# An mLSTM cell followed by a gated feed-forward: the second product of two of four batches by seven half-width block products in place of eight

## The chip, the core and the metric

The kernel runs on one core of one Trainium2 chip. The metric is device time in microseconds of one launch. Before the change three runs took 549.52, 550.34 and 550.58 us, a median of 550.34 us. The profiled execution spans 549.5 us with a mean granted TensorE clock of 0.993.

## What is computed

There are four batches, eight heads, 768 time steps and a head size of 40. An mLSTM cell gives, for each batch and time step, a row of 8 x 40 = 320 numbers. These 3072 rows then go through a feed-forward with 2048 inner units, and this second part is what the change is about:

```python
# x: 3072 x 320, w_in: 320 x 2048, w_out: 2048 x 320, all float32
h = x @ w_in
g = h * np.cos(h)
return (g @ w_out).astype(np.float32)
```

## The kernel before, in words

**Chunks and blocks.** Time is cut into six chunks of 128 steps (`NC = 6`, index `c`). A chunk of one batch is a tile of 128 rows, so a chunk has four tiles, one per batch. The 2048 inner units are sixteen blocks of 128 (`NF = 16`), taken two at a time (`f2` from 0 to 7, `e` = 0 and 1 within a pair).

**First product.** `Up(c, f2)` computes h for one pair of blocks and all four batches, transposed: 128 inner units on the partitions and 4 x 128 time steps along the free axis. Each of the two blocks fills one PSUM bank of 512 float32, of which there are two in the pool `ps_u`, so the next `Up` needs both back. From these banks ScalarE rounds (`near`, L621), VectorE takes the rest (`rest`, L624), ScalarE takes the sine (`sin`, L629), and VectorE multiplies (`gate`, L633). The result `gs[c, 2 * f2 + e]` is a 128 x 512 tile in SBUF: inner units by (batch, time). The factor of two pi and the cosine are folded into the scaling.

**Second product.** `down(c, f2)` (L637 to L649) adds, for both blocks of a pair, g times w_out to the four output tiles of the chunk. Each output tile of one batch is 128 time steps by 320 columns and sits in a PSUM bank of its own for the whole chunk (`po[c]`, pool `ps_o`, four banks). A call is eight matmuls: for each block and batch, the 128 x 128 slice of g is the stationary operand and the 128 x 320 block of w_out the moving one. In the last call of a chunk (f2 = 7) the eight are sorted by batch, and each finished bank is copied by ScalarE to SBUF (L648, tile `o_sb`, two buffers) and sent out by DMA (L649).

**Order of the work.** The order on every engine is the program's order; it is written by hand in `both_parts(c, b)` (L789 to L899), called for each chunk and each b from 0 to 3. A call has two halves. The first half issues `Up(c, 2b)`, then pieces of the mLSTM cell of the next chunk (scores, weights, the exponents `decay_exponents` for the cell after that, the exponential `decay`), and then `down` of the pair before. The second half issues `Up(c, 2b + 1)`, the end of the cell, and `down(c, 2b)`. So each `down` is issued one half later than its `Up`. The last pair of chunk c - 1 is done in the first half of `both_parts(c, 0)`, and for the last chunk after the loops (L907).

Within a first half the queues hold, in this order: ScalarE `near`, `sin`, the exponential of `decay` (L379), then the output copies of `down` if it closes a chunk; VectorE `rest`, `weigh` (L451), the subtraction of `decay_exponents` (L370), `gate`, later `normalize_turned`; GpSimd the selection of `decay_exponents` (L371), on which the exponential of `decay` waits, and `weigh_k` (L392); TensorE `Up`, `scores` (L445), `down`, `values_turned` (L482, L488), then the next `Up`. From chunk 5 on there are no cells left, and a half holds `Up` and `down` alone.

**Weights.** w_in and w_out arrive as 64-bit floats and are converted in chunk 0, by `parts` on ScalarE and `join` on VectorE and GpSimd. The tiles `bits` (pools `pb` and `pc`) and `wt` (pool `p2`) serve that conversion and lie idle afterwards.

Of the kernel before, what the change touches and what calls it, by code (L numbers as in the profile page):

```python
# [11 lines left out]
FP = mybir.dt.float32  # L12
# [4 lines left out]
OP = mybir.AluOpType  # L17
# [12 lines left out]
def kernel(  # L30
# [20 lines left out]
    nc = tc.nc  # L51

    B, H, S, D = q.shape
    C = 128
# [4 lines left out]
    DM = H * D  # L59
    DFF = moe_w_in.shape[1]  # L60
    NF = DFF // 128
# [13 lines left out]
    p2 = ctx.enter_context(tc.tile_pool(name="p2", bufs=2))  # L75
    p3 = ctx.enter_context(tc.tile_pool(name="p3", bufs=3))
    p4 = ctx.enter_context(tc.tile_pool(name="p4", bufs=4))
    pb = ctx.enter_context(tc.tile_pool(name="pb", bufs=5))
    pc = ctx.enter_context(tc.tile_pool(name="pc", bufs=3))
# [3 lines left out]
    ps_o = ctx.enter_context(tc.tile_pool(name="ps_o", bufs=4, space=bass.MemoryType.PSUM))  # L83
# [15 lines left out]
    p1 = ctx.enter_context(tc.tile_pool(name="p1", bufs=1))  # L99
# [20 lines left out]
    w_out_sb = wp.tile([128, NF, DM], FP, name="w_out_sb")  # L120
# [11 lines left out]
    def parts(dst, bits):  # L132
        n = dst.shape[1]
        hi, lo = bits[:, 0:n, 1], bits[:, 0:n, 0].bitcast(U32)
        t = p2.tile([128, WQ], I32, name="wt", tag="wt")[:, 0:n]
        m = p2.tile([128, WQ], I32, name="wm", tag="wm")[:, 0:n]

        nc.scalar.activation(out=t.bitcast(FP), in_=hi.bitcast(FP), func=AF.Abs)

        nc.scalar.activation(out=m, in_=lo, func=AF.Copy, scale=2.0 ** -29)  # L140
        return dst, hi, t, m
# [164 lines left out]
    def sigmoid(c, bs=slice(0, B)):  # L306
        o = sig[c][:, bs.start * DM:bs.stop * DM]
        nc.scalar.activation(out=o, in_=o, func=AF.Sigmoid)
# [51 lines left out]
    def psum_o():  # L360
        return ps_o.tile([128, HP, C], FP, name="pm", tag="o")

    def cols(n, j, width):
        c, b = divmod(n, B)
        return tab[:, c, j, ts(b, H)].unsqueeze(2).to_broadcast([128, H, width])


    def decay_exponents(n):
        E = Es[n]
        nc.vector.tensor_tensor(out=E, in0=E, in1=cols(n, 0, C), op=OP.subtract)  # L370
        nc.gpsimd.affine_select(out=E, in_=E, compare_op=OP.is_ge, fill=1.0e30, base=0,  # L371
                                pattern=[[0, H], [1, C]], channel_multiplier=-1)
# [5 lines left out]
    def decay(n):  # L378
        nc.scalar.activation(out=Es[n], in_=Es[n], func=AF.Exp, scale=-1.0)  # L379
# [9 lines left out]
    def weigh_k(n):  # L389
        if n < N - B:  # L390
            kw = p2.tile([128, H, D], FP, name="kw", tag="kw")
            nc.gpsimd.tensor_tensor(out=kw, in0=ks[n % NB][:, :, 0:D], in1=cols(n, 1, D), op=OP.mult)  # L392
            kws[n] = kw
# [44 lines left out]
    def scores(n):  # L438
        pool, tag = psum(n)
        qT, kT = qkT[n]  # L440
        ps = [pool.tile([128, HP, C], FP, name="ps", tag=tag) for _ in range(2)]
        for p in range(HP):
            for j in range(2):
                r = slice(64 * j, 64 * j + (64 if n < TURNED else D))
                nc.tensor.matmul(ps[j][:, p], kT[r, p], qT[r, p], start=True, stop=True)  # L445
        pss[n] = ps

    def weigh(n):
        for j in range(2):
            w = Es[n].rearrange("p (a j) t -> p a j t", j=2)[:, :, j]  # L450
            nc.vector.tensor_tensor(out=w, in0=pss[n][j], in1=w, op=OP.mult)  # L451

    def values_kept(n):

        pool, tag = (ps_o, "o") if n == B else psum(n)
        heads_of[n] = None
        if n >= B:
            pq = pool.tile([128, H, D1], FP, name="pq", tag=tag)
            for p in range(HP):
                nc.tensor.matmul(pq[:, 2 * p:2 * p + 2].rearrange("p j d -> p (j d)"), qkT[n][0][:, p],  # L460
                                 st[n % B][:, p].rearrange("p j d -> p (j d)"), start=True, stop=True)
            heads_of[n] = pq
# [136 lines left out]
    gs, po = {}, {}  # L599

    class Up:
# [29 lines left out]
        def gate(self, e):  # L631
# [2 lines left out]
                                           op0=OP.mult, op1=OP.mult)  # L634
            gs[self.c, 2 * self.f2 + e] = g

    def down(c, f2):  # L637
        if f2 == 0:
            po[c] = [ps_o.tile([128, DM], FP, name="po", tag="o") for _ in range(B)]

        order = [(f, b) for f in (2 * f2, 2 * f2 + 1) for b in range(B)]
        if f2 == NF // 2 - 1:
            order.sort(key=lambda fb: fb[1])
        for f, b in order:
            nc.tensor.matmul(po[c][b], gs[c, f][:, ts(b, C)], w_out_sb[:, f], start=(f == 0), stop=(f == NF - 1))  # L645
            if f == NF - 1:
                o = p2.tile([128, DM], FP, name="o_sb", tag="o_sb")
                nc.scalar.copy(out=o, in_=po[c][b])  # L648
                nc.sync.dma_start(out=out[b * S + c * C:b * S + (c + 1) * C], in_=o)  # L649


    pw, pmu = (ps_u.tile([128, HP, C], FP, name=name, tag="up") for name in ("pw", "pmu"))
# [1 line left out]
    def warm(k, bank=None):  # L654

        for _ in range(k):
            nc.tensor.matmul(bank or pw, nil, nil.unsqueeze(1).to_broadcast([128, HP, 128]), start=True, stop=True)
# [122 lines left out]
    def out_parts():  # L780
        p, piece = outs.pop(0)
        return p, parts(*piece)

    def out_join(p, h, last=None):
        join(*h, last)
        if p + 3 < NF // 2:
            outs.append((p + 3, weights_out(p + 3)))

    def both_parts(c, b):  # L789

        n = (c + 1) * B + b
        cell = n < N
        begin = c == b == 0
        more = cell and n + 1 < N
        f2 = 2 * b
        up = Up(c, f2)
        if cell:  # L800
            scores(n)
            if begin:
                values_kept(n)

                warm(6, psum_o())
        for e in range(2):
            up.near(e)
        if begin:
            weigh(n)
        for e in range(2):  # L810
            up.rest(e)
        if cell and not begin:
            weigh(n)
        if begin or more and c > 0:
            decay_exponents(n + 1)
        for e in range(2):
            up.sin(e)
            up.gate(e)
        if c == 0 and b == 1:
            sigmoid(1, slice(1, B))  # L820
        if b == B - 1 and c + 2 < NC:
            sigmoid(c + 2)
        h = ()
        if begin:
            h = out_parts()
            w = parts(*pieces.pop(0))
        else:
            if c == 0:
                out_join(*out_parts())
            if pieces:  # L830
                join(*parts(*pieces.pop(0)))
        if begin or more and c > 0:
            decay(n + 1)
        elif more:
            decay_by_bias(n + 1)
        if f2 > 0:
            down(c, f2 - 1)
        elif c > 0:
            down(c - 1, NF // 2 - 1)
        if cell:  # L840
            if n + 2 < N:
                load(n + 2)
            if n < TURNED:
                if not begin:
                    values_kept(n)
                values(n)
                normalize(n)
            else:
                values_turned(n)
            if begin:  # L850
                out_join(*h, nc.vector)
            if TURNED <= n + 2 < N:
                load_G(n + 2)
            if n + 3 < N:
                load_E(n + 3)
            if b == B - 2 and c + 2 < NC:
                load_o(c + 2)
            if n >= TURNED:
                normalize_turned(n)
            fade(n)  # L860
        h = w if begin else ()
        if not begin:
            sin_next()
        if pieces and not begin:
            h = parts(*pieces.pop(0))
        up = Up(c, f2 + 1)
        if cell:
            seam(n)
        for e in range(2):
            up.near(e)  # L870
        for e in range(2):
            up.rest(e)
        if cell and n < TURNED:
            seam_out(n)
        if h:
            join(*h)
        if cell:
            state(n)
        for e in range(2):
            up.sin(e)  # L880
            up.gate(e)
        if more:
            weigh_k(n + 1)
        if pieces:
            join(*parts(*pieces.pop(0)))
        down(c, f2)
        if pieces:
            join(*parts(*pieces.pop(0)))
        if c == 0:
            if b + 2 < B:  # L890
                pieces.extend(weights_in(b + 2))
            h = out_parts()
        if more and n + 1 < TURNED:
            turn(n + 1)
            turn_out(n + 1, c > 0)
        elif more:
            turn_blocks(n + 1)
        if c == 0:
            out_join(*h)  # L899
# [38 lines left out]
```

## Time and profile before

| what | value |
|---|---|
| TensorE busy | 538.8 us of the 549.5 |
| VectorE busy | 355.9 us |
| ScalarE busy | 264.4 us |
| GpSimd busy | 76.7 us |
| matmul records at L645 (the second product) | 768 |
| matmul records at L613 and L616 (the first product) | 384 and 192 |
| first and last copy of an output tile, L648 | 143.8 and 545.6 us |
| output copies of chunks 1, 2, 3 begin | 228.41, 312.92, 397.43 us |

The profile gives for each engine the time that it was busy, for each source line the instructions and their mean duration, and, in the timeline, runs of equal instructions with the start, the time from the first start to the last end, and how many there were. "PE" is TensorE's matmuls and "PEld" its weight loads, "DVE" is VectorE, "ACT" ScalarE, "POOL" GpSimd. The second product has 16 blocks x 24 tiles = 384 matmuls in the program and 768 records: each float32 matmul is recorded as two passes, each with a weight load of its own. Durations of matmuls overlap, since they are pipelined; the distance from one start to the next is what a pass costs in a full stream.

### The profile page before, as it was taken

The page shows a single profiled execution, that of the slowest core. Times are in us where ns is not written, and L with a number is a line of the kernel's source. Part 1 is how long each engine was busy: PE and PEld are TensorE (multiplying, and loading weights), DVE is VectorE, ACT ScalarE, POOL GpSimd, SP SyncE. Part 2 cuts the span into 40 slices and gives each one's busy share as a digit, 9 for nine tenths or more (in the row PEclk, how much of TensorE's full clock was granted, in tenths as well). Part 3 has the DMA queues.
Part 4 walks back from the last instruction along what each step waited for, and adds up shares of the span by engine and source line. Part 5 has one row for each costly group of instructions (what it writes and reads, how often), then busy time and mean ns, then how long its engine had stood idle before and what let it go on. Part 6 is the DMA issues. An engine that isn't in the chain of part 4 may idle for free.

```text
span 549.5 us, 9153 instructions
## 1 busy us (share of the span) xinstructions
PE 538.8 (98%) x3395; PEld 317.4 (58%) x3395; DVE 355.9 (65%) x692; ACT 264.4 (48%) x420; POOL 76.7 (14%) x112
## 2 busy tenths in 40 slices
PE   9989899999999999999999999999999999999997
PEld 6865566665565565565565555555655655555554
DVE  5876987968777677677667667667666665232311
ACT  4868795775632544543435344427335323331312
POOL 5531433523110100101101101100000000000000
PEclk9979999999999999999999999999999999999999
DMA  9999985851265651166625076635075000100001
GB/s 143 206 226 221 239 220 145 189 124 33 77 142 129 148 124 36 50 136 138 151 75 107 26 158 139 143 78 110 4 173 109 8 14 12 51 1 1 0 0 50
DMA packets 134509, 56.83 MB, mean 103 GB/s; under 512 B 72080, under 2 KB 130528, under 8 KB 134464
## 3 DMA queue, kind: packets, MB, share of 16 engines
q1 hardware_dynamic: 134320, 56.04, 46.0%
q8 instruction: 27, 0.44, 0.3%
q0 software_dynamic: 96, 0.18, 0.2%
q14 instruction: 18, 0.15, 0.1%
q10 hardware_dynamic: 48, 0.02, 0.0%
HBM read 50.00 MB, written 6.21 MB: 102 GB/s over the span
## 4 chain that ended last, share of the span: by engine, by line
PE 85%; DVE 5%; DMA 4%; SPq 3%; POOL 1%; ACT 1%; issue 1%; DVEq 0%; ACTq 0%; POOLq 0%
PE po L645 37%; PE pup L613 28%; PE pup L616 8%; PE hp L488 3%; PE ps L445 3%; PE hp L482 2%; PE pu L580 1%; DMA E<-M_d 1%; SPq L327 1%; PE pt L426 1%; SPq L129 1%; DMA qs<-in_q_dram 1%; DMA bits<-in_moe_w_out_dram 1%; DMA M_d<-M_rows 1%; DMA bits<-in_moe_w_in_dram 1%
## 5 line engine op out<-in xcount | busy, mean ns | idle before, releaser
L645 PE MATMUL po<-w_out_sb,g 128*128 128x320 f32 x768 | 219.3, 439 | 1.3 <-POOL w_out_sb L149 1.0
L645 PEld LDWEIGHTS po<-w_out_sb,g 128*128 128x128 f32 x768 | 142.0, 190 | 67.0 <-issue 8.3
L613 PE MATMUL pup<-xT,w_in_sb 128*128 128x512 f32 x384 | 175.5, 599 | 0.9 <-POOL w_in_sb L149 0.6
L621 ACT ACTIVATE n<-pup 128x512 int32<-128x512 f32 x96 | 52.0, 593 | 214.3 <-PE pup L616 214.3
L624 DVE SCALAR_TENSOR_TENSOR n<-pup,n 128x512 f32<-128x512 f32 x96 | 61.9, 686 | 135.1 <-ACT n L621 135.0
L613 PEld LDWEIGHTS pup<-xT,w_in_sb 128*128 128x128 f32 x384 | 71.2, 191 | 77.6 <-issue 63.9
L629 ACT ACTIVATE n<-n 128x512 f32<-128x512 f32 x96 | 58.8, 630 | 12.1 <-DVE n L624 12.1
L633 DVE SCALAR_TENSOR_TENSOR g<-pup,n 128x512 f32<-128x512 f32 x96 | 61.7, 685 | 1.7
L371 POOL TENSOR_SCALAR_AFFINE_SELECT E<-E 128x1024 f32<-128x1024 f32 x19 | 20.8, 1094 | 292.9 <-DVE E L370 273.6
L616 PE MATMUL pup<-xT,w_in_l 64*128 64x512 f32 x192 | 54.2, 641 | 0.0
L616 PEld LDWEIGHTS pup<-xT,w_in_l 64*128 64x128 f32 x192 | 14.4, 184 | 36.4 <-issue 35.6
L451 DVE TENSOR_TENSOR E<-ps,E 128x512 f32<-128x512 f32 x48 | 30.7, 680 | 6.1 <-PE ps L445 6.1
L379 ACT ACTIVATE E<-E 128x1024 f32<-128x1024 f32 x21 | 22.2, 1058 | 21.7 <-POOL E L371 17.2
L410 DVE STREAM_TRANSPOSE t<-qs 128x512 f32<-128x512 f32 x32 | 32.3, 1087 | 0.0
L445 PEld LDWEIGHTS ps<-t,t 40*128 40x128 f32 (+1 forms) x384 | 25.1, 188 | 9.7 <-issue 8.9
L445 PE MATMUL ps<-t,t 40*128 40x128 f32 (+1 forms) x384 | 25.8, 274 | 0.0
L370 DVE TENSOR_TENSOR E<-E,tab 128x1024 f32<-128x1024 f32 x19 | 23.1, 1216 | 0.4 <-DMA E<-M_d 0.4
L379 ACT ACT_TABLE_LOAD x18 | 23.1, 1283 | 0.3
L778 ACT ACT_TABLE_LOAD x18 | 23.1, 1283 | 0.3
L502 DVE STREAM_TRANSPOSE room<-hp 128x128 f32<-128x128 f32 x32 | 8.6, 306 | 22.5 <-PE hp L488 22.5
L488 PE MATMUL hp<-E,vs 128*32 128x128 f32 x512 | 17.3, 276 | 0.0
L417 DVE STREAM_TRANSPOSE room<-o 128x256 f32<-128x256 f32 x32 | 17.2, 618 | 0.0
(128 smaller groups left out, 428.9 us busy)
## 6 DMA issues: line engine op xcount, KB each, us to landing
E<-M_d SPq DMA_DIRECT2D x22, 512.0 KB
bits<-in_moe_w_in_dram SPq DMA_DIRECT2D x40, 128.0 KB
bits<-in_moe_w_out_dram SPq DMA_DIRECT2D x8, 640.0 KB
room<-G_d SPq DMA_DIRECT2D x32, 128.0 KB
ks<-in_k_dram SPq DMA_DIRECT2D x24, 160.0 KB
vs<-in_v_dram SPq DMA_DIRECT2D x24, 160.0 KB
out_dram<-o_sb SPq DMA_DIRECT2D x24, 160.0 KB
qs<-in_q_dram SPq DMA_DIRECT2D x32, 80.0 KB
```

Source lines behind the costliest of these rows:

```text
L379: nc.scalar.activation(out=Es[n], in_=Es[n], func=AF.Exp, scale=-1.0)
L410: nc.vector.transpose(out=dst.rearrange("r p (t x) -> r p x t", x=T4), in_=src.rearrange("r p (x d) -> r p x d", x=T4)[:, :, :, 0:32])
L445: nc.tensor.matmul(ps[j][:, p], kT[r, p], qT[r, p], start=True, stop=True)
L451: nc.vector.tensor_tensor(out=w, in0=pss[n][j], in1=w, op=OP.mult)
L488: nc.tensor.matmul(hps[n][j][ts(p, 32), half], vs[n % NB][:, h, lo:lo + DA], Es[n][:, h], start=False, stop=True, skip_group_check=True)
L613: nc.tensor.matmul(pu, w_in_sb[:, i, ts(block(f2, e), 128)], x(i), start=(i == 0), stop=False)
L616: nc.tensor.matmul(pu, w_in_l[r, f2], x(NK, r), start=False, stop=True)
L621: nc.scalar.activation(out=self.n[e], in_=self.pu[e], func=AF.Copy, bias=0.25)
L624: nc.vector.scalar_tensor_tensor(out=self.n[e].bitcast(FP), in0=self.pu[e], scalar=0.25, in1=self.n[e], op0=OP.add, op1=OP.subtract)
L629: nc.scalar.activation(out=r, in_=r, func=AF.Sin, scale=TWO_PI_DOWN)
L633: nc.vector.scalar_tensor_tensor(out=g, in0=self.pu[e], scalar=TWO_PI, in1=self.n[e].bitcast(FP), op0=OP.mult, op1=OP.mult)
L645: nc.tensor.matmul(po[c][b], gs[c, f][:, ts(b, C)], w_out_sb[:, f], start=(f == 0), stop=(f == NF - 1))
```

## The change

For two of the four batches (b = 0 and 1), the two blocks of a pair and the two column halves of w_out form a product of 2 x 2 blocks by 2 x 2 blocks: A is g of two batches (rows) and two inner blocks, B is w_out of two inner blocks and two halves of 160 columns. Instead of eight block products the new code computes seven, of sums of blocks of A with sums of blocks of B, and combines the seven in a closing step. A matmul of the old kind covers both column halves, so in matmuls the four of 320 columns for these two batches become seven of 160 columns. Batches 2 and 3 stay with whole products, and chunk 0 stays as it was (`parted`).

- `sums(c, f2)`: four sums and differences of 128 x 128 slices of g, on GpSimd, after the gates of each pair, into a tile of the tag `wt`.
- `two_differences`, `differences`: four differences of 128 x 160 halves of w_out for each of the eight pairs, on GpSimd, once, from the end of chunk 0 to the third call of chunk 1, in the tiles of the tag `bits`.
- `down_parted(c, f2)`: the new second product. The seven running sums of products lie in PSUM as follows: `Ps[0..2]` in the first bank, `Ps[3..5]` in the second, `Ps[6]` at columns 320 to 479 of the third, whose columns 0 to 319 hold batch 2; batch 3 has the fourth. Except in the closing call of a chunk, the whole products come first and the seven follow. In the closing call the seven come first, in the order 0, 1, 3, 4, 5, 6, 2; then ScalarE copies `Ps[0]` to SBUF, VectorE adds and subtracts in seven instructions of 128 x 160, the two outputs are sent, and the whole products of batches 2 and 3 with their copies come last.

The purpose is fewer columns to stream through TensorE: 7 x 160 in place of 4 x 320 for each pair of blocks.

```diff
+    def differences(p, T):
+        B11, B12, B21, B22 = (w_out_sb[:, 2 * p + e, ts(h, DH)] for e in range(2) for h in range(2))
+        for i, (x, y) in enumerate(((B12, B11), (B22, T[:, 0]), (B22, B12), (T[:, 1], B21))):
+            nc.gpsimd.tensor_tensor(out=T[:, i], in0=x, in1=y, op=OP.subtract)
+        Ts[p] = T
...
+    def sums(c, f2):
+        if not parted(c):
+            return
+        S = p2.tile([128, 4, C], FP, name="sg", tag="wt")
+        A11, A21, A12, A22 = (gs[c, 2 * f2 + e][:, ts(b, C)] for e in range(2) for b in range(2))
+        for i, (x, y, op) in enumerate(((A21, A22, OP.add), (S[:, 0], A11, OP.subtract),
+                                        (A11, A21, OP.subtract), (A12, S[:, 1], OP.subtract))):
+            nc.gpsimd.tensor_tensor(out=S[:, i], in0=x, in1=y, op=op)
+        sg[c, f2] = S
+
+    def down_parted(c, f2):
+        end = f2 == NF // 2 - 1
+        if f2 == 0:
+            po[c] = [ps_o.tile([128, 3 * DH + 32], FP, name="po", tag="o") for _ in range(4)]
+        banks = po[c]
+        Ps = [banks[i // 3][:, ts(i % 3, DH)] for i in range(6)] + [banks[2][:, DM:DM + DH]]
...
+        def product(out, g, w, first):
+            nc.tensor.matmul(out, g, w, start=(f2 == 0 and first), stop=end, skip_group_check=True)
+
+        def whole():
+            for b in range(2, B):
+                for e, (g, w) in enumerate(((g0, w0), (g1, w1))):
+                    product(banks[b][:, 0:DM], g[:, ts(b, C)], w, e == 0)
+                if end:
+                    o = p2.tile([128, DM], FP, name="o_sb", tag="o_sb")
+                    nc.scalar.copy(out=o, in_=banks[b][:, 0:DM])
+                    result(c, b, o)
+
+        if not end:
+            whole()
+        product(Ps[0], g0[:, 0:C], w0[:, lo], True)
+        product(Ps[1], g1[:, 0:C], w1[:, lo], False)
+        product(Ps[3], g1[:, C:2 * C], T[:, 3], True)
+        product(Ps[4], S[:, 0], T[:, 0], False)
+        product(Ps[5], S[:, 1], T[:, 1], False)
+        product(Ps[6], S[:, 2], T[:, 2], False)
+        product(Ps[2], S[:, 3], w1[:, hi], False)
+        if end:
+            o0, o1 = (p2.tile([128, DM], FP, name="o_sb", tag="o_sb") for _ in range(2))
+            U = p1.tile([128, 2, DH], FP, name="hs", tag="hs")
+            nc.scalar.copy(out=U[:, 0], in_=Ps[0])
+            for dst, x, y, op in ((o0[:, lo], U[:, 0], Ps[1], OP.add), (U[:, 0], U[:, 0], Ps[5], OP.add),
+                                  (U[:, 1], U[:, 0], Ps[6], OP.add), (U[:, 0], U[:, 0], Ps[4], OP.add),
+                                  (o0[:, hi], U[:, 0], Ps[2], OP.add), (o1[:, lo], U[:, 1], Ps[3], OP.subtract),
+                                  (o1[:, hi], U[:, 1], Ps[4], OP.add)):
+                nc.vector.tensor_tensor(out=dst, in0=x, in1=y, op=op)
+            for b, o in enumerate((o0, o1)):
+                result(c, b, o)
+            whole()
...
     def down(c, f2):
+        if parted(c):
+            down_parted(c, f2)
+            return
...
         for e in range(2):
             up.sin(e)
             up.gate(e)
+        sums(c, f2)
...
+        sums(c, f2 + 1)
         if more:
             weigh_k(n + 1)
+        if c == 0 and b == B - 1 or c == 1 and b < B - 1:
+            two_differences(c * (2 * b + 2))
```

More of the change, by code (lines that the diff above doesn't have):

```diff
@@ L635, in gate, with parted, two_differences @@
             gs[self.c, 2 * self.f2 + e] = g
+    DH = DM // 2
+    Ts, sg = {}, {}
+    def parted(c):
+        return c > 0
+    def differences(p, T):
[3 more added lines that the diff above has]
+        Ts[p] = T
+    def two_differences(p):
+        if p < 6:
+            T = pc.tile([128, 2, 4, DH], FP, name="T", tag="bits")
+            for e in range(2):
+                differences(p + e, T[:, e])
+        else:
+            for e in range(2):
+                differences(p + e, pb.tile([128, 4, DH], FP, name="T", tag="bits"))
@@ new lines, in down_parted @@
+    def down_parted(c, f2):
[4 more added lines that the diff above has]
+        Ps = [banks[i // 3][:, ts(i % 3, DH)] for i in range(6)] + [banks[2][:, DM:DM + DH]]
+        g0, g1 = (gs[c, 2 * f2 + e] for e in range(2))
+        w0, w1 = (w_out_sb[:, 2 * f2 + e] for e in range(2))
+        S, T = sg[c, f2], Ts[f2]
+        lo, hi = slice(0, DH), slice(DH, DM)
+        def product(out, g, w, first):
[29 more added lines that the diff above has]
+            whole()
@@ L637, in down, with result @@
+    def result(c, b, o):
+        nc.sync.dma_start(out=out[b * S + c * C:b * S + (c + 1) * C], in_=o)
     def down(c, f2):
+        if parted(c):
+            down_parted(c, f2)
+            return
         if f2 == 0:
@@ L648, in down @@
                 nc.scalar.copy(out=o, in_=po[c][b])
-                nc.sync.dma_start(out=out[b * S + c * C:b * S + (c + 1) * C], in_=o)
+                result(c, b, o)
     pw, pmu = (ps_u.tile([128, HP, C], FP, name=name, tag="up") for name in ("pw", "pmu"))
```

## The prediction, made before the changed kernel ran

> **What bounds the kernel now.** I read the share of busy time first, then the groups by line and shape, then the timeline of a plain half, of the last pair, and of the half where a chunk closes.
>
> ```profile
> PE 538.8 (98%) x3395; PEld 317.4 (58%) x3395; DVE 355.9 (65%) x692; ACT 264.4 (48%) x420; POOL 76.7 (14%) x112
> ...
> L645 PE MATMUL po<-w_out_sb,g 128*128 128x320 f32 x768 | 219.3, 439 | 1.3 <-POOL w_out_sb L149 1.0 <-DVE w_out_sb L149 0.3
> ```
>
> TensorE is busy all the time and idles 1.3 us ahead of the second product in the whole run. It is the bound, so a column less is time less and a wait on TensorE is time more. What a pass costs comes from the timeline of TensorE:
>
> ```profile
> 20.07 1.98 PE L470 MATMUL ph<-vs,E 128*128 128x41 f32 x16
> ...
> 486.98 3.60 PE L613 MATMUL pup<-xT,w_in_sb 128*128 128x512 f32 x8
> ...
> 491.57 4.57 PE L645 MATMUL po<-w_out_sb,g 128*128 128x320 f32 x16
> ...
> 534.54 1.02 PE L613 MATMUL pup<-xT,w_in_sb 128*128 128x512 f32 x2
> ...
> 536.55 8.88 PE L645 MATMUL po<-w_out_sb,g 128*128 128x320 f32 x32
> ```
>
> Sixteen more passes of 320 columns take 8.88 - 4.57 = 4.31 us, or 0.269 each. Six more of 512 take 3.60 - 1.02 = 2.58, or 0.430. That is 0.839 ns a column with almost no fixed part. The 16 passes of 41 columns take (1.98 - 0.28) / 15 = 0.113 each[...]. The first pass of a run costs 0.10 more (4.57 - 15 x 0.269 - 0.43).
>
> Now the half in which chunk 1 closes, `both_parts(2, 0)`, all engines:
>
> ```profile
> 222.57 1.29 DVE L624 SCALAR_TENSOR_TENSOR n<-pup,n 128x512 f32<-128x512 f32 x2 [2.79 <-ACT n L621]
> 222.67 4.57 PE L645 MATMUL po<-w_out_sb,g 128*128 128x320 f32 x16
> 223.77 1.28 DVE L451 TENSOR_TENSOR E<-ps,E 128x512 f32<-128x512 f32 x2
> 224.97 1.22 DVE L370 TENSOR_TENSOR E<-E,tab 128x1024 f32<-128x1024 f32 x1
> 226.10 1.28 DVE L633 SCALAR_TENSOR_TENSOR g<-pup,n 128x512 f32<-128x512 f32 x2
> 226.32 1.09 POOL L371 TENSOR_SCALAR_AFFINE_SELECT E<-E 128x1024 f32<-128x1024 f32 x1 [19.40 <-DVE E L370]
> 227.18 0.67 PE L482 MATMUL hp<-room,st 40*32 40x128 f32 x32
> 227.45 1.06 ACT L379 ACTIVATE E<-E 128x1024 f32<-128x1024 f32 x1 [1.63 <-POOL E L371]
> 228.41 0.73 ACT L648 COPY o_sb<-po 128x320 f32<-128x320 f32 x2
> 228.78 1.12 PE L613 MATMUL pup<-xT,w_in_sb 128*128 128x512 f32 x2
> ```
>
> The output copies (L648) start at 228.41, not when their matmuls end: ScalarE waits for GpSimd's selection and runs the exponential L379 first. Today that costs nothing: no matmul waits for these copies until the next half. The same order recurs with copies at 312.92 and 397.43.
>
> [...] No tile of the kernel before shares a bank between sums that end at different times, so its trace doesn't show such a wait. [...] After an idle of 1.59 us behind thin matmuls the granted clock falls, and it stays down for 6.8 us (columns: window; then for each stage its length, the busy times, the clock, the DMA share, GB/s):
>
> ```profile
> 32.75:33.00 0.25, 0.00 (x0) 0.00 (x0) 0.25 (x1) 0.20 (x2) 0.00 (x0) 0.89 1.04 114
> 33.00:33.25 0.25, 0.00 (x0) 0.00 (x0) 0.21 (x2) 0.25 (x1) 0.00 (x0) 0.50 1.48 145
> 39.50:39.75 0.25, 0.25 (x2) 0.07 (x1) 0.00 (x0) 0.25 (x1) 0.25 (x1) 0.50 0.91 348
> 39.75:40.00 0.25, 0.25 (x2) 0.17 (x1) 0.00 (x0) 0.25 (x2) 0.25 (x2) 0.96 1.09 414
> ```
>
> [...] The gates (L633) have one input in PSUM, and their duration is 680 to 693 ns in all 66 records from 137 to 480 us, with GpSimd at work beside some. I charge nothing.
>
> **The change part by part.**
>
> *Ordinary calls (35 of the 40 new ones).* Out go 8 passes of 320 columns, 8 x 0.269 = 2.152. In come 14 of 160. No row has 160; from 320, 0.269 - 160 x 0.839 / 1000 = 0.135, take 0.136. The lower bound is the floor of 0.113, the upper 0.19, the mean duration of a weight load, if loads were not hidden. I take 0.136 since passes of 41 columns already run at 0.113 with loads. 14 x 0.136 = 1.904, so a call gains 0.248. All but one of the 35 count here: 34 x 0.248 = 8.4. The last stands with the tail.
>
> *Sums on GpSimd.* No row has 128 columns. The 40 x 164 tensor_tensor (L565) takes about 0.465, the 128 x 320 (L392) 0.723, so 128 is about 0.41, with the gap of 0.07 between two in a row 0.48; four are 1.9 us. After the gates (227.38) they are ready at 229.3, and the next `down` that needs them starts at 233.91: hidden. In chunk 5 they are ready at 487.9 (gates end at 485.98); the products that need them start at about 493.8. The differences, 8 x 0.53 = 4.2 us four times, fall into GpSimd's long idle times (19 us before L371) and are needed a half later: hidden. `weigh_k` goes back by 1.9 us and has a half to spare.
>
> *The gates' slack.* The next `Up` waits for both gates. In chunk 5 they end at 494.97 and the next `Up` starts at 495.98; 0.25 less leaves 0.76. In the other chunks the second half leaves about 0.9 (237.39 against 238.32). Enough.
>
> *The closing calls.* Here is the new wait. The first whole matmul (batch 2) writes the bank where `Ps[6]` lies, and VectorE reads `Ps[6]` in its third instruction. So the whole matmul has to wait for ScalarE's copy of `Ps[0]` and three VectorE instructions. Behind it on TensorE are eight whole passes, `values_turned`, and the next `Up`, for which `near` on ScalarE and all that follows wait.
>
> In `both_parts(2, 0)`: products from 222.67, issued until 222.67 + 0.10 + 1.904 = 224.67. ScalarE's copy is behind the exponential and starts at 228.41. Its size: 128 x 320 takes 0.426 (L648), 128 x 512 takes 0.593 (L621), so 160 is 0.287, and it ends at 228.70. VectorE: 128 x 256 from PSUM takes 0.395 (L511), 128 x 512 takes 0.680 (L451), so 160 is 0.288, with gaps 0.30; from 228.74 three end at 229.64. TensorE goes on at 229.70. The last of eight whole passes starts at 229.70 + 7 x 0.269 = 231.58. Before, the last pass started at 222.67 + 0.10 + 15 x 0.269 = 226.81, and `Up` 1.97 later. So the next `Up` is at 233.55 in place of 228.78: +4.8. Three closings (chunks 1 to 3) have this order: +14.4. The close of chunk 4, `both_parts(5, 0)`, has no cell: products from 482.57 to 484.57, gates until 485.98, three instructions until 486.90, whole passes from 486.95, next `Up` at 489.1 against 486.98: +2.1.
>
> *The tail.* The last gates end at 540.02, the sums at 541.95. The last ordinary call ends at 536.55 + 0.10 + 8 x 0.269 + 1.904 = 540.71. The products run until 542.62 with no wait (`S[:, 3]` is needed at 542.35). The last ends 0.16 after its stream, at 542.78; copy until 543.11; three instructions until 544.05; whole passes 544.1 to 546.4. The output copies of batches 2 and 3 reuse the two buffers, so batch 3's waits until the DMA of `o1` has landed: seven instructions end at 545.25, the DMA takes 1.8 (as the one issued at 543.76), the copy runs 547.1 to 547.55. Before, the last copy ended at 546.07, 3.4 us ahead of the end. So +1.5.
>
> *The clock.* TensorE idles 224.95 to 229.70, 4.75 us, in three closings. [...] Half-clock work of 2 to 5 us costs half of it, 1.0 to 2.6; I take 1.5 each, 4.5. The idle of 2.4 us in the close of chunk 4 may or may not do it: 0.8. None for the tail (1.3 us of idle).
>
> Sum: -8.4 + 14.4 + 2.1 + 1.5 + 4.5 + 0.8 = +14.9, so 550.3 becomes 565 us.
>
> **Rivals.** *No wait at the close*: whole passes go on beside VectorE's reads. For it: the addresses differ. [...] Then 38 calls gain 0.248, 9.4, and the tail still loses 1.5 to the buffers: 542.4, faster. *The wait, with the clock kept*: 550.3 - 8.4 + 14.4 + 2.1 + 1.5 = 560. *A longer wait*, until all seven VectorE instructions are done: 4 x 0.30 = 1.2 more in five closings, 571. *Passes dearer than 0.136*: at 0.15, 40 x 14 x 0.014 = 7.8 more, 573; at 0.19, 595. Against it: the row of 41 columns.
>
> **How the numbers follow.** Wait with halved clock 0.62 (565), wait with full clock 0.14 (560), longer wait 0.08 (571), dearer passes 0.04 (573 and up), no wait 0.12 (542). The predicted time is the first. The range 556 to 572 takes in the first three with their error: 0.5 for each of three closings, and 1.0 to 2.6 for each clock drop. Faster is the no-wait case, 0.12; the same 0.02; slower 0.86.
>
> **What would show it.** Right: 160-column passes 0.136 apart; the closing whole matmul waiting for VectorE, 4 to 5 us at chunks 1 to 3; the copy of `Ps[0]` straight behind L379; granted clock 0.5 just after; 21 us between ordinary calls of `both_parts` becoming 20.6. Wrong: whole matmuls straight behind the products at the close, GpSimd's sums named as what TensorE waits for, or passes over 0.14.

## The result, and the profile after

The changed kernel takes 567.73 us (median of 4 runs, 566.48 to 569.53) against 550.46 us of the kernel before. The ratio is 1.0318, 95% interval 1.0286 to 1.035: slower by 3.2%. The profiled execution spans 564.5 us against 549.5.

The page of the changed kernel: busy time by engine, then two of its groups by line (busy time, mean ns of one, and after the last bar the idle time ahead of the group with what ended it).

```profile
PE 535.8 (95%) x3635; PEld 337.3 (60%) x3635; DVE 367.1 (65%) x727; ACT 262.0 (46%) x415; POOL 166.9 (30%) x304
...
L689 PE MATMUL po<-w_out_sb,g 128*128 128x320 f32 (+1 forms) x480 | 125.7, 412 | 18.7 <-DVE hs L717 18.7
...
L672 POOL TENSOR_TENSOR sg<-g 128x128 f32<-128x128 f32 x80 | 36.5, 457 | 217.6 <-DVE g L633 216.2
```

TensorE is busy for 535.8 us, less than before, and yet the span is longer: ahead of the second product it now idles 18.7 us where it idled 1.3, and all of it ends with an instruction of VectorE at L717, the combining of the seven sums. GpSimd's sums and differences more than double its busy time, and no matmul is named as waiting for them.

The timeline of the changed kernel, all engines, in the half that closes chunk 1 (start and length in us, engine, line, names, shape, count, and in brackets the idle time before with its releaser):

```profile
220.37 0.98 PE L689 MATMUL po<-T,sg 128*128 128x160 f32 x6
...
221.18 0.43 PE L689 MATMUL po<-w_out_sb,sg 128*128 128x160 f32 x2
...
222.87 1.28 DVE L633 SCALAR_TENSOR_TENSOR g<-pup,n 128x512 f32<-128x512 f32 x2
223.09 1.09 POOL L371 TENSOR_SCALAR_AFFINE_SELECT E<-E 128x1024 f32<-128x1024 f32 x1 [6.65 <-DVE E L370]
224.22 1.06 ACT L379 ACTIVATE E<-E 128x1024 f32<-128x1024 f32 x1 [1.62 <-POOL E L371]
...
225.18 0.27 ACT L712 COPY hs<-po 128x160 f32<-128x160 f32 x1
...
225.49 0.32 DVE L717 TENSOR_TENSOR o_sb<-hs,po 128x160 f32<-128x160 f32 x1 [1.33 <-ACT hs L712]
...
225.84 1.03 DVE L717 TENSOR_TENSOR hs<-hs,po 128x160 f32<-128x160 f32 x3
...
226.58 4.53 PE L689 MATMUL po<-w_out_sb,g 128*128 128x320 f32 x8 [4.96 <-DVE hs L717]
...
232.64 3.70 PE L613 MATMUL pup<-xT,w_in_sb 128*128 128x512 f32 x8
```

The products end at 221.6. The copy of `Ps[0]` stands behind GpSimd's selection and the exponential L379 and starts at 225.18. VectorE follows, and the whole products start 4.96 us after the last product. The passes of 160 columns run (0.98 - 0.30) / 5 = 0.136 us apart. The eight whole passes take 4.53 us from the first start to the last end, where 7 x 0.269 + 0.43 = 2.31 is my estimate for full clock, from the spacing and the last pass before. The granted clock of the same stretch says why (columns: window; then its length, the busy time of the five engines, the clock, the DMA share, GB/s):

```profile
222.00:225.00 3.00, 0.00 (x0) 0.00 (x0) 2.16 (x3) 1.38 (x2) 1.71 (x3) 0.84 0.00 0
225.00:228.00 3.00, 1.42 (x3) 1.03 (x4) 2.07 (x7) 0.46 (x2) 1.12 (x3) 0.50 0.00 0
228.00:231.00 3.00, 3.00 (x7) 1.47 (x5) 0.00 (x0) 0.42 (x1) 0.00 (x0) 0.52 0.47 164
231.00:234.00 3.00, 3.00 (x68) 1.89 (x68) 1.30 (x6) 1.91 (x3) 0.00 (x0) 1.00 0.37 102
```

Where the time went, in the two profiles. The marks are the starts of the L616 matmuls in the timeline; each stage is the difference of two marks.

| stage | calls | before, us | after, us | difference | predicted |
|---|---|---|---|---|---|
| start to the first mark of chunk 1 | no new ones | 136.17 | 134.70 | -1.47 | 0 |
| the five stretches between closings | 34 ordinary | 355.23 in all | 346.68 | -8.55 | -8.4 |
| close of chunk 1 | 1 | 11.70 | 18.78 | +7.08 | +6.3 |
| close of chunk 2 | 1 | 11.70 | 18.24 | +6.54 | +6.3 |
| close of chunk 3 | 1 | 11.69 | 19.52 | +7.83 | +6.3 |
| close of chunk 4 | 1 | 9.00 | 11.38 | +2.38 | +2.9 |
| last mark to the end | 1 ordinary, the last close | 14.00 | 15.23 | +1.23 | +1.5 |
| sum | 40 | 549.5 | 564.5 | +15.0 | +14.9 |

The first row belongs to no edit: apart from eight differences on GpSimd at its end, the code of that stage is the old one, and in the six experiments, where it is the same too, the stage takes from 134.46 to 136.59 us. TensorE waits there for a DMA at L426, 1.59 us in the profile before and 0.79 us in this one, and the granted clock is 0.50 from 32.94 us on for 6.8 us in the one, from 32.89 us on for 3.4 in the other. So the sum of +15.0 meets the forecast of +14.9 in part by luck: without start-up it is +16.5. The four runs of the changed kernel span 564.5 to 567.5 us, and the profiled one is the shortest.

### The profile page after: what moved, and what is told of

It reads as the page before. It is cut to its first block, busy times and chain, and to the rows that moved or that the text cites. A ratio compares the mean times of both kernels' runs of the same rounds, so it can differ in the third digit from the quotient of the medians.

```text
span 564.5 us, 9948 instructions
## 1 busy us (share of the span) xinstructions
PE 535.8 (95%) x3635; PEld 337.3 (60%) x3635; DVE 367.1 (65%) x727; ACT 262.0 (46%) x415; POOL 166.9 (30%) x304
## 4 chain that ended last, share of the span: by engine, by line
PE 80%; DVE 8%; SPq 3%; DMA 3%; POOL 2%; ACT 2%; issue 1%; DVEq 0%; POOLq 0%; ACTq 0%
PE po L689 30%; PE pup L613 28%; PE pup L616 8%; PE po L736 4%; PE hp L488 3%; PE ps L445 3%; PE hp L482 2%; SPq L129 1%; DVE n L624 1%; PE pu L580 1%; DMA vs<-in_v_dram 1%; SPq L327 1%; DVE g L633 1%; DMA qs<-in_q_dram 1%; DVE E L370 1%
## 5 line engine op out<-in xcount | busy, mean ns | idle before, releaser
L689 PE MATMUL po<-w_out_sb,g 128*128 128x320 f32 (+1 forms) x480 | 125.7, 412 | 18.7 <-DVE hs L717 18.7
L689 PEld LDWEIGHTS po<-w_out_sb,g 128*128 128x128 f32 x480 | 86.3, 196 | 57.9 <-DVE hs L717 19.9
L613 PEld LDWEIGHTS pup<-xT,w_in_sb 128*128 128x128 f32 x384 | 69.8, 190 | 74.3 <-issue 63.7
L672 POOL TENSOR_TENSOR sg<-g 128x128 f32<-128x128 f32 x80 | 36.5, 457 | 217.6 <-DVE g L633 216.2
L616 PE MATMUL pup<-xT,w_in_l 64*128 64x512 f32 x192 | 54.2, 641 | 0.0
L689 PE MATMUL po<-T,sg 128*128 128x160 f32 x240 | 39.2, 299 | 0.0
L736 PE MATMUL po<-w_out_sb,g 128*128 128x320 f32 x128 | 36.6, 439 | 1.3 <-POOL w_out_sb L149 1.0
L616 PEld LDWEIGHTS pup<-xT,w_in_l 64*128 64x128 f32 x192 | 14.5, 185 | 36.4 <-issue 35.6
L689 PEld LDWEIGHTS po<-T,sg 128*128 128x128 f32 x240 | 34.8, 190 | 0.0
L379 ACT ACTIVATE E<-E 128x1024 f32<-128x1024 f32 x21 | 22.2, 1057 | 22.6 <-POOL E L371 21.3
L736 PEld LDWEIGHTS po<-w_out_sb,g 128*128 128x128 f32 x128 | 23.7, 190 | 11.0 <-POOL w_out_sb L149 1.3
```

Of the source, the lines that this page charges most:

```text
L613: nc.tensor.matmul(pu, w_in_sb[:, i, ts(block(f2, e), 128)], x(i), start=(i == 0), stop=False)
L616: nc.tensor.matmul(pu, w_in_l[r, f2], x(NK, r), start=False, stop=True)
L672: nc.gpsimd.tensor_tensor(out=S[:, i], in0=x, in1=y, op=op)
L689: nc.tensor.matmul(out, g, w, start=(f2 == 0 and first), stop=end, skip_group_check=True)
```

## The experiments

All times are medians beside runs of the kernel before on the same chip: 550.09 us for e1 to e4, 550.14 us for e5 and e6.

### e1_whole_first: no matmul behind the shared bank

In closing calls, too, the whole products come first; the copies of batches 2 and 3 stay last.

```diff
-        if not end:
-            whole()
+        whole()
...
             for b, o in enumerate((o0, o1)):
                 result(c, b, o)
-            whole()
+            copies()
```

> The changed kernel, but in the closing call of a chunk, too, the whole products of batches 2 and 3 come first; the seven products, VectorE's seven instructions and the copies follow, so no matmul waits behind a read of a shared bank. Nothing is left out. Theory (the wait at the five closings is the loss): no idle of TensorE over 0.5 us at the closings and no halved clock there; 38 calls x 0.248 = 9.4 us gained, 1.6 to 1.9 lost in the tail, since the seven VectorE instructions now come after the last matmul, and at most 0.5 where they delay the gates: about 543 us (541 to 546). Rival (the loss lies in the ordinary calls: dearer passes, or GpSimd's sums in the way): 558 us or more. Second rival (the wait only moves, from the shared bank to the next first product, whose gates VectorE finishes late): about 548 us.

Measured: 546.58 us (9 runs, 545.1 to 549.89), ratio 0.9935 (0.9916 to 0.9955); the profiled span is 543.0 us. The timeline of e1_whole_first where chunk 1 closes:

```profile
223.08 0.43 PE L689 MATMUL po<-w_out_sb,sg 128*128 128x160 f32 x2
223.45 0.67 PE L482 MATMUL hp<-room,st 40*32 40x128 f32 x32
...
224.93 0.27 ACT L713 COPY hs<-po 128x160 f32<-128x160 f32 x1
...
225.06 3.70 PE L613 MATMUL pup<-xT,w_in_sb 128*128 128x512 f32 x8
225.24 0.32 DVE L718 TENSOR_TENSOR o_sb<-hs,po 128x160 f32<-128x160 f32 x1 [1.33 <-ACT hs L713]
```

ScalarE and VectorE come just as late as in the changed kernel, but TensorE has gone on. By the same marks the four closings of chunks 1 to 4 now take 0.25 us less than before each, in place of 2.4 to 7.8 more. So the wait, with what follows it, is the loss of these closings, and the ordinary calls are sound. The median is over the range that I gave, for two reasons in the profile. The stretches right behind the closings of chunks 1 to 3 take 0.90, 0.25 and 0.23 us longer than in the changed kernel, where I had allowed 0.5 in all; in the first of them TensorE waits 0.63 us for a gate that comes late. And the tail loses 3.4 us in place of 1.6 to 1.9: from the last mark to the end it takes 17.4 us, before 14.0. The end of the same timeline:

```profile
534.61 0.43 PE L689 MATMUL po<-w_out_sb,sg 128*128 128x160 f32 x2
...
539.06 0.90 ACT L699 COPY o_sb<-po 128x320 f32<-128x320 f32 x2 [3.69 <-DMA out_dram<-o_sb]
```

The copies of batches 2 and 3 wait for the DMAs of batches 0 and 1 to give their buffers back, 4 us after the last matmul. I had charged VectorE's seven instructions, but not this wait of the copies for a DMA, and not the DMA behind the copies. (Start-up, 134.46 us here, hides 1.7 us of this in the profiled span.)

### e2_batch3_ahead: which bank it is

```diff
-            for b in range(2, B):
+            for b in ((3, 2) if end else (2, 3)):
```

> The changed kernel, but in the closing call batch 3, which shares no bank with the seven products, comes ahead of batch 2, which does. Nothing is left out. Theory (the wait is one for the bank of Ps[6], and for no other): the four passes of batch 3 run at once, so four closings save 4 x 0.269 = 1.08 us each and the tail next to nothing: about 563 us (561 to 565[...]). Rival (TensorE waits at the close whatever the bank, for the tiles as a group or for VectorE in general): no change, 567 to 568 us, and the idle still in front of the first whole matmul.

Measured: 562.12 us (561.14 to 563.44), ratio 1.021 (1.0185 to 1.0234). TensorE's timeline of e2_batch3_ahead:

```profile
223.32 1.24 PE L689 MATMUL po<-w_out_sb,g 128*128 128x320 f32 x4
228.44 1.53 PE L689 MATMUL po<-w_out_sb,g 128*128 128x320 f32 x4 [3.88 <-DVE hs L717]
```

Batch 3, with no other sum in its bank, runs straight behind the products, 0.27 us after the start of the last one. Batch 2 waits as before, and the idle is 3.88 us, less by just the 1.08 us of batch 3. So the wait is for the one bank in which `Ps[6]` lies beside batch 2, though the columns differ. What is called a bank here is one tile of the program, 128 x 512 float32, so the run does not tell a wait for the bank from a wait for the tile.

### e3_filled_wait: the clock by itself

Seventeen matmuls that nobody reads fill the wait in three closings; they leave its end where it is.

```diff
+        if end and c < NC - 2:
+            for _ in range(17):
+                nc.tensor.matmul(banks[3][:, DM:DM + DH], ident, w0[:, lo], start=False, stop=False, skip_group_check=True)
```

> The changed kernel with 17 more float32 matmuls of 160 columns, 34 passes, behind the seven products of the closings of chunks 1 to 3; they write columns of batch 3's bank that nobody reads. They fill 34 x 0.136 = 4.6 us of the 4.96 us wait and leave its end where it is. Theory (the halved clock is a cost of its own beside the wait): the clock stays at 1.0 at these three closings and 6.8 us come back, the halves of 4.3, 3.2 and 6.1 us of half-clock work in the profile of the changed kernel: about 561 us (559.5 to 563). Rival (the clock matters little, the wait alone is the loss): no gain, 566 to 568 us.

Measured: 563.03 us (559.61 to 563.95), ratio 1.0209 (1.0167 to 1.0252): 4.7 us back by the medians, and just over my range. TensorE's timeline of e3_filled_wait, and then its clock:

```profile
223.12 4.78 PE L711 MATMUL po<-w_out_sb,ident 128*128 128x160 f32 x34
228.25 2.42 PE L689 MATMUL po<-w_out_sb,g 128*128 128x320 f32 x8 [0.34 <-DVE hs L720]
```

```profile
225.00:228.00 3.00, 2.90 (x22) 2.66 (x20) 1.60 (x5) 1.24 (x2) 2.60 (x5) 1.00 0.00 0
```

The clock stays at 1.00, the whole passes take 2.42 us in place of 4.53, and each of these three closings costs 4.98 us more than before, in place of 7.08, 6.54 and 7.83. So the bare wait costs 3 x 4.98 = 14.9 us in the profile, and the halved clock behind it 21.4 - 14.9 = 6.5. The medians differ by less than that. In this profile the clock also fell at the close of chunk 4, after 2.36 us of idle that had no such effect in the changed kernel's profile, so that closing costs +4.1 in place of +2.4, and start-up took 136.35 us in place of 134.70.

### e4_no_sums: GpSimd's sums

As e1_whole_first, but without the four sums of g for each pair; the products that use them read plain slices of g, so the output is another one.

```diff
     def sums(c, f2):
-        if not parted(c):
-            return
+        return
...
-        S, T = sg[c, f2], Ts[f2]
+        S, T = g0.rearrange("p (i t) -> p i t", i=4), Ts[f2]
```

> As e1_whole_first, but the four sums of g on GpSimd are left out, and the products that use them read plain slices of g; the output is another one. Theory (the sums are hidden): the same time as e1_whole_first within 0.7 us. Rival (GpSimd's 160 instructions more slow VectorE or hold up TensorE): faster than e1_whole_first by 1.5 us or more.

Measured: 546.0 us (10 runs, 543.56 to 549.77), ratio 0.9919 (0.9895 to 0.9942), against 546.58 and 0.9935 of e1_whole_first. The intervals overlap, and the profiled spans are 543.2 and 543.0 us. From the first mark of chunk 1 to the last one, the kernel without sums is 0.7 us shorter, nearly all of it in the one chunk where e1_whole_first waits for a gate. That the sums cost something between 0 and 0.7 us there is open; that they are the loss is excluded.

### e5_copy_before_exp: what sets the end of the wait

In closing calls the exponential L379 is issued behind the copy of `Ps[0]`: the call of `down` gets `decay(n + 1)` as `then`.

```diff
-        if begin or more and c > 0:
+        closing = b == 0 and c > 1
+        if (begin or more and c > 0) and not closing:
             decay(n + 1)
...
             nc.scalar.copy(out=U[:, 0], in_=Ps[0])
+            if then:
+                then()
```

> The changed kernel, but in a closing call ScalarE's exponential of the next cell's weights is issued behind the copy of Ps[0] in place of ahead of it. Nothing is left out. Theory (the end of the wait is set by ScalarE's queue, behind which VectorE's is next): the copy starts when the products are done, VectorE starts right behind its gates, in the close of chunk 1 at 224.18 in place of 225.49, so TensorE goes on 1.3 us earlier in three closings: about 563.8 us (561.5 to 566[...]), idle 3.6 us in place of 4.96. Rival (VectorE alone sets it, by the gates and its own seven instructions): no change, idle still 4.9 us.

Measured: 560.62 us (559.44 to 564.64), ratio 1.0216 (1.0175 to 1.0257). The timeline of e5_copy_before_exp where chunk 1 closes:

```profile
222.36 0.29 ACT L712 COPY hs<-po 128x160 f32<-128x160 f32 x1 [0.36 <-PE po L689]
...
223.58 1.28 DVE L633 SCALAR_TENSOR_TENSOR g<-pup,n 128x512 f32<-128x512 f32 x2
224.78 0.31 DVE L719 TENSOR_TENSOR o_sb<-hs,po 128x160 f32<-128x160 f32 x1
...
225.86 3.97 PE L689 MATMUL po<-w_out_sb,g 128*128 128x320 f32 x8 [3.54 <-DVE hs L719]
```

Now the copy starts with the end of the products, and VectorE's gates are what the combining stands behind. The idle falls by 1.4 us, from 4.96 to 3.54, in all three closings. So ScalarE's queue did set the end, with VectorE's gates next. The median is 0.9 us under my range, and in the profile the clock accounts for it: it fell for 3.4 us at two of the three closings and not at all at the other, against 6.8, 3.4 and 6.8 us in the changed kernel. The three closings gain 7.5 us, 4.3 from the wait and the other 3.2 from the clock.

### e6_no_wait: the seven products without the wait

From e1_whole_first and e5_copy_before_exp, and in the last closing `Ps[6]` gets a bank of the pool `ps_a`, which is free by then, so that the whole products run beside VectorE's instructions; the outputs of batches 0 and 1 get tiles of their own.

```diff
+        if c == NC - 1:
+            if f2 == 0:
+                extra.append(ps_a.tile([128, DH], FP, name="pe", tag="a"))
+            Ps[6] = extra[0]
...
-        if not end:
-            whole()
+        last = end and c == NC - 1
+        if not last:
+            whole()
...
-            o0, o1 = (p2.tile([128, DM], FP, name="o_sb", tag="o_sb") for _ in range(2))
+            o0, o1 = (p1.tile([128, DM], FP, name=t, tag=t) for t in "yz")
```

> The seven products without the wait, as a version to keep: in closings of chunks 1 to 4 the whole products first and the exponential behind the copy of Ps[0]; in the last closing, where a bank is free, Ps[6] lies in a bank of its own, and the whole products run beside VectorE's seven instructions; the outputs of batches 0 and 1 go to tiles of their own, so no copy waits for a DMA. Nothing is left out. Theory: all 39 calls before the last gain 0.248, 9.7 us, and the tail is no longer than before (13.5 us from the last first-product group to the end, before 14.0): about 540.3 us (539 to 542). Rival (a shorter second product makes the gates the bound, as the 0.63 us wait for a gate in e1_whole_first hints): 543 us or more, with waits of TensorE for L633.

Measured: 541.01 us (540.49 to 542.23), ratio 0.9839 (0.9821 to 0.9856): faster than the kernel before by 1.6%, and than the changed one by 26.7 us. The page of e6_no_wait:

```profile
PE 528.3 (98%) x3635; PEld 334.1 (62%) x3635; DVE 368.7 (68%) x727; ACT 261.9 (49%) x415; POOL 167.0 (31%) x304
```

TensorE is busy 98% of the span again, with 10.5 us less to do. By the marks, chunks 1 to 5 up to the last mark gain 9.55 us in 38 calls, 0.251 a call, and the tail takes 13.96 us against 14.00.

## Why the prediction was right

I forecast 565.0 us in a range of 556 to 572, and 567.73 us were measured. By its own steps:

- **Ordinary calls, -8.4.** Measured -8.55. The pass of 160 columns, interpolated at 0.136 us, runs at 0.136. What sets the 0.113 us of the 41-column passes, my lower bound, no run shows.
- **Sums and differences on GpSimd, hidden.** Right within what e4_no_sums can tell. A sum takes 0.457 us in place of my 0.41. Four are through 1.9 us after the gate, as reckoned: behind the gates in the half that closes chunk 4 they run from 490.19 to 492.0. One reading was wrong and cost nothing: `weigh_k` goes back not by 1.9 us but by 12, since it now stands behind the sums of the second half as well, which wait for that half's gates. In the first call of chunk 1 it starts 18.6 us after the first mark, before 6.6.
- **The closing calls.** That a whole matmul waits for the reading of other columns of its bank was an assumption of mine: nothing in the profile before showed it. The cause is the one forecast: e1_whole_first takes it away, e2_batch3_ahead ties it to the one bank. My 4.8 us for each of three is 4.98 in e3_filled_wait, where the clock plays no part. The copy took 0.27 us, near my 0.287; VectorE's instructions started 0.35 apart in place of 0.30. The close of chunk 4: +2.4, where I had 2.1 with 0.8 for the clock, which didn't fall in this profile.
- **The queue that sets the end.** Forecast as ScalarE's, with the exponential ahead of the copy. e5_copy_before_exp shows it: 1.4 us less idle where I said 1.3 ahead of that run.
- **The clock.** Right in kind, too small in size: 4.5 us charged for three closings, 6.5 measured (the difference between the changed kernel's profile and e3_filled_wait). The low clock lasted 6.8, 3.4 and 6.8 us, of which TensorE worked 4.3, 3.2 and 6.1. I had taken 3 us of half-clock work for each, an estimate that no trace had shown; the low stretch that I had from the kernel before was 6.8 us long. This is the mis-sized term of the sum. That the length of the idle decides was an assumption too. The fall that I had shown from the kernel before came 0.60 us into an idle of 1.59 us (from 32.34 us on; the clock falls at 32.94), and the one in e3_filled_wait came with 2.36 us, an idle that no fall followed in the changed kernel's profile. The last section has what the traces show.
- **The tail, +1.5.** Measured +1.23.

Start-up adds -1.47 to the profiled difference, which no step of mine contains. Without it the profiled difference would be 16.5 us, near the 17.3 of the medians.

Of the rivals, the one without a wait falls with the first profile. The one with the clock kept is what e3_filled_wait builds, 563.03 us against my 560 for it, with one clock drop at a closing left in it. The longer wait falls: TensorE goes on after the third VectorE instruction, while four are still to come. Passes were not dearer.

## What to carry to other kernels

Before a sum is put into the free part of a PSUM bank, ask who will read it and what TensorE writes to that bank next. Here a read on a slow queue became a wait of TensorE of 4.96 us at the close of chunk 1. Its length was that of the queues ahead of the read, not of the reads themselves, three instructions of 0.32 us: with the exponential behind the copy it was 3.54 us (e5_copy_before_exp). Fewer columns paid here once the reads fell behind the last write of each bank. The same seven products were 3.2% slower with the whole products behind them, 0.65% faster with the whole products in front (e1_whole_first), and 1.6% faster when ScalarE's order, the bank of the last closing and the output tiles were changed as well (e6_no_wait).

## What the runs showed that I had not expected

- The granted clock after an idle of TensorE varied, also for idles of one length. After 4.96 us of idle, in the changed kernel, it was at 0.50 for 3.4 or 6.8 us; after 3.88 us, in e2_batch3_ahead, for 3.4, 6.8 and 3.4; after 3.54 us, in e5_copy_before_exp, twice for 3.4 and once not at all. After 2.36 us it fell in one of the three profiles that show the close of chunk 4 with this idle, after 1.45 us in none.
- In the changed kernel's profile the low stretches begin at 32.89, 224.03, 316.19 and 404.94 us: the last three 56, 83 and 109 times 3.413 us behind the first, and they last 3.413 or 6.827 us. So I cut the span into stretches of 3.413 us from these marks and took TensorE's idle time in each (the ends of matmuls are modelled there, so the figures are rough). In the changed kernel it idled 2.42, 3.41 and 3.41 us in the stretches right ahead of the falls at 224.03, 316.19 and 404.94. In stretches at closings that no fall followed it idled 1.33 us (from 309.37 on), 0.78 (from 398.11), 1.59 (from 486.86) and 1.45 (from 555.13). Of the low stretches themselves, the two that lasted 3.4 us (from 32.89 and 316.19 on) had 0.21 us of idle each, and in the two of 6.8 us TensorE idled 2.55 and 0.76 us of the first half. These are the figures of this profile. The same columns as above, first two stretches at the second closing of e5_copy_before_exp (its 3.54 us of idle lie in both, 1.66 and 1.87, and no fall follows), then two at the third closing of e2_batch3_ahead (busy for 1.38 us, idle for 2.03, and the clock falls):

```profile
308.50:311.91 3.41, 1.75 (x13) 1.50 (x12) 3.41 (x6) 2.80 (x4) 0.18 (x1) 1.00 0.00 0
311.91:315.32 3.41, 1.54 (x6) 1.15 (x7) 2.85 (x9) 1.06 (x1) 2.64 (x5) 1.00 0.00 0
...
403.54:406.95 3.41, 1.38 (x12) 0.79 (x20) 2.06 (x7) 0.91 (x2) 1.49 (x4) 1.00 0.00 0
406.95:410.37 3.42, 3.42 (x65) 2.40 (x64) 0.80 (x3) 2.13 (x3) 0.00 (x0) 0.50 0.53 184
```

In start-up, among thin matmuls, the clock fell behind stretches with 0.57 us of idle (the changed kernel, 29.47 to 32.88) and 0.60 us (the kernel before, 29.53 to 32.94), but not behind one with 0.98 us (the changed kernel, 63.61 to 67.02) or 0.80 us (the kernel before, 67.08 to 70.49). So idle time in such a stretch does not decide alone there, and no run tells what does.

- GpSimd's `weigh_k` (L392, 128 x 320) takes 0.72 us before and 1.17 us in the eleven calls of the changed kernel from chunk 1's first call on. There it runs beside VectorE's L413 for 0.58 to 0.64 us and beside L417 for about 0.8 us; before, it ran beside neither. L413 itself takes 0.71 us in the mean in these calls, 0.68 before, but also 0.71 in its four later calls with no L392 beside it. In e1_whole_first, with the sums, L392 takes 1.17 us too; in e4_no_sums, the same order without them, it is back at 0.725. By what the sums lengthen it, no run shows. No matmul waits for it, and the ordinary calls of e6_no_wait, where it takes 1.17 as well, still gain their full 0.25 us.
